# Fourier mixing and a SwiGLU block on one core: the inverse transform's last step by whole blocks of 96 rows, and weight rounding packed into five sixths of each group

## The chip, the cores and the metric

The kernel runs on one core of a Trainium2 chip. The metric is the device time of one execution in microseconds (us). The kernel before takes 2937.25 us, the median of three runs (2936.93 to 2938.33). The profile is of one such execution, with a span of 2935.5 us.

Engines are named as in the profile: PE is TensorE's matmul, PEld its weight load, DVE is VectorE, ACT is ScalarE, POOL is GpSimd, SP is SyncE, which only issues transfers here.

## The reference

Eight batches of 3008 tokens with 256 channels are filtered in the frequency domain along the tokens, and the result goes through a gated feed-forward block.

```python
# x (8, 3008, 256), filt_r and filt_i (1505, 256), all float32
X = np.fft.rfft(x, axis=1)
Y = X * (filt_r + 1j * filt_i)[None]
y = np.fft.irfft(Y, n=3008, axis=1).astype(np.float32)

x2 = y.reshape(24064, 256)
g, val = x2 @ w_gate, x2 @ w_val              # 256 -> 1536
out = ((g / (1 + np.exp(-g))) * val) @ w_out  # 1536 -> 256
```

The weights w_gate, w_val and w_out come as 64-bit floats. The kernel has to turn them into 32-bit floats on the chip, with integer operations on their two halves; its code calls this rounding.

## The kernel before

**Order of work.** The feed-forward part of a batch is 12 steps: 4 chunks of tokens times 3 groups of hidden blocks. One step is one pass through a list of 150 tokens. A token is one small operation, such as a product (P, Q, A, B, E), a copy (m, c, f), a gate (g, u, h, v), a projection (W) or its addition to the output (o). A prime marks work of the group before. The tokens `t0.0` to `t4.2'` advance pieces of the next batch's transforms.

```python
SCHEDULE = """
Q0 o3' t4.2' W2 f0 S00' S01' x0.o' t0.0 x1.o' Q1 t0.1 x2.o' P3 x3.o' f1 t4.3' W1 x4.o' S10' x03 S11'
s13 x5.o' P1 o1 t0.2 P0 o2 c1 D01 A13 g1 c0 S20' Q2 S21' g0 y01 m13 t1.0 h0 f2 s01 W6 t1.1 h1 x23
D02 P2 o6 D12 A01 c2 B13 g2 n3' m01 t0.3 S30' t1.2 x02 W7 S31' g13 y12 y02 B01 h13 o7 t1.3 t2.0 s02
s12 g01 h2 Q3 t2.1 h01 e12 A02 y23 W4 e02 y03 m02 g3 A12 o4 t2.2 E12 m12 B02 t2.3 l12 E02 u12 e13
g02 t3.0 h3 s23 l02 B12 v12 E13 t3.1 h02 u02 A23 n2 l13 g12 v02 W5 s03 e23 h12 e01 m23 A03 o5 u13
E23 t3.2 m03 v13 E01 l23 e03 t3.3 t4.0 l01 u23 B23 v23 u01 t4.1 E03 n1 v01 g23 B03 l03 W3 h23 g03
u03 h03 v03
""".split()
```

Counted from 0, P0 is place 27, A01 place 52, E01 place 127 and v03 place 149. The operations D01, D02, D12 are subtractions on POOL; n2 and n1 make sums for the next chunk on POOL.

**Rounding in the first batch.** All rounding, and the making of further weights as sums of rounded ones, is cut into ticks, numbered 0 to 170. 45 of them are done before the first step. The others are spread over the tokens of the first steps of batch 0. A tick has a few operations: some on DVE and ACT, those on POOL marked below. `finish` runs at the start of a step whatever ticks the step needs that are not yet done.

```python
# round_half(i): one half block of weights
#  n=0 DVE L322 | n=1 DVE L325, ACT L327 | n=2, 3, 4 ACT L330, L332, L334
#  n=5 DVE L337 | n=6 DVE L341
#  n=7 POOL: product with the power of two (L349 into wo_t, or L361 and L362)
#  n=8 POOL: for an output weight, four subtractions
for n, t in enumerate((0, 1, 2, 3, 4, 6, 7, 9, 10)):
    put(b + t, go, by, n > 6)          # b is 48 for the last half that step 1 needs
...                                    # sums of weights for six pairs:
for n, pair in enumerate(PAIRS_USED):  # DVE or ACT, then POOL
    for t in range(3):
        put(b + 11 + n + t, lambda c=c: next(c, None), by if g or n < 4 else 1, t == 2)
```

```python
TICKS = 20
for place, token in enumerate(SCHEDULE):                      # 150 places
    if b == 0 and this and place * TICKS % len(SCHEDULE) < TICKS and \
            (step or place > SCHEDULE.index("A01")):
        preparation.tick(step)
```

The projection `W2` of a step's group stands at place 3 of the next step. Its second half reads the rounded output weights `wo_t` and the last product of the hidden layer, `v03` at place 149.

**The transforms' last step.** A transform along 3008 = 47 x 64 tokens has three stages. Stage 2 leaves its result in DRAM (`d2`), and stage 3 loads it back as `t4` and multiplies it by a small table. One call of `stage3` handles 4 columns of 64 (`NH` = 4) and half of the channels (`cb`), so a chunk has 4 calls and a batch 16. In batch 0 a call is four matmuls over 96 rows with 94 outputs each. From batch 1 on, the rows are stored token by token and packed over 128 partitions, and a call is three matmuls with 141, 188 and 141 outputs.

```python
# L696, batches 1 to 7                       BACK has 3, 4 and 3 pieces of 47 columns
for j in range(len(BACK) if back else 0):
    cols = back_t[0][:, first:first + N1 * len(BACK[j])]
    ...
    pin(nc.tensor.matmul(out=rows, lhsT=self.t4[k, i][:, j, ts(cb, 128)], rhs=cols,
                         start=j == 0, stop=True, skip_group_check=True))
# L699, batch 0
for n in range(0 if back else NH):
    pin(nc.tensor.matmul(out=psv[:, n, :], lhsT=self.t4[k, i][0:NK, n, ts(cb, 128)],
                         rhs=wi_t, start=n == 0, stop=True, skip_group_check=True))
```

```python
# load_t4
t = t4pool.tile([128, NH, C], FP32, ...)
if self.b == 0:
    self.load(out=t[0:NK], in_=self.d2_rows[:, ts(at, NH), :])
else:
    ...
    for j in range(2):
        self.load(out=t[64 * j:64 * j + 64, 1], in_=rows[j, 128 * (1 - j):128 * (1 - j) + 64])
        self.load(out=t[:, 2 * j], in_=rows[j, 64 * j:64 * j + 128])
# stage2b
if self.b == 0:
    pin(queue.dma_start(out=self.twos(self.d2, u), in_=g))
    return
rows = self.d2_tokens.rearrange("n (p s) c -> (n p) (s c)", p=2)
pin(queue.dma_start(out=rows[:, ts(u, NV * C)], in_=g.rearrange("q s c -> q (s c)")))
```

Of the kernel before, what the change touches and what calls it, by code (L numbers as in the profile page):

```python
# [56 lines left out]
NK = 4 * NS  # L57
# [55 lines left out]

BACK = (((0, 0, 0, 48), (1, 48, 0, 48), (2, 96, 0, 32)),
        ((4, 64, 0, 48), (5, 112, 0, 16), (2, 0, 32, 16), (3, 16, 0, 48)),
        ((5, 0, 16, 32), (6, 32, 0, 48), (7, 80, 0, 48)))
BACK_AT = (0, 3 * N1, 7 * N1)


def dft_tables():
    n1, n2 = np.arange(N1), np.arange(N2)
    s, q = np.arange(NS), np.arange(NQ)
    ph = 2 * np.pi * (np.outer(n1, s) % N1) / N1
    w = np.stack([np.cos(ph), -np.sin(ph)], 1)
    wf = np.zeros((N1, 2, NS, 2, 2))
    wi = np.zeros((NS, 2, 2, N1, 2))

    v = np.stack([2 * np.cos(ph), -2 * np.sin(ph)], 0)  # L130
    v[0, :, 0], v[1, :, 0] = 1.0, 0.0
    for h in range(2):
        wf[:, h, :, :, h] = w.transpose(0, 2, 1)
        wi[:, :, h, :, h] = v.transpose(2, 0, 1) / S
    one = wi[:, :, 0, :, 0].transpose(1, 0, 2).reshape(2 * NS, N1)
    back = np.zeros((128, 10 * N1))
    for tile_, first in zip(BACK, BACK_AT):
        for i, (_, row, a, rows) in enumerate(tile_):
            back[row:row + rows, first + N1 * i:first + N1 * (i + 1)] = one[a:a + rows]


    kap = np.where(q[:, None] < 32, s + N1 * q[:, None], s + N1 * (95 - q[:, None]))
    sg = np.where(q < 32, 1.0, -1.0)[:, None]
    th = 2 * np.pi * ((n2[:, None, None] * kap) % S) / S
    c, sn = np.cos(th), np.sin(th)
    d = np.zeros((2, N2, NS, 2, NQ))
    d[0, :, :, 0] = c.transpose(0, 2, 1)
    d[1, :, :, 0] = sn.transpose(0, 2, 1)
    d[0, :, :, 1] = (-sn * sg).transpose(0, 2, 1)
    d[1, :, :, 1] = (c * sg).transpose(0, 2, 1)  # L150
    d = d.reshape(128, NS, 128)
    de = np.stack([d, d.transpose(2, 1, 0)], 2)

    pairs = np.arange(128).reshape(2, N2).T.ravel()
    later = np.stack([de[:, :, 0], de[:, :, 1][:, :, pairs]], 2)
    f32 = np.float32
    return (wf.reshape(NR, NK).astype(f32), wi.reshape(NK, NR).astype(f32),
            back.astype(f32), np.ascontiguousarray(de).astype(f32),
            np.ascontiguousarray(later).astype(f32))
# [3 lines left out]
def kernel(  # L163
# [11 lines left out]
    wf_host, wi_host, back_host, de_host, later_host = dft_tables()  # L175
    wf_dram = nc.inline_tensor(wf_host, name="wf_tbl")
    wi_dram = nc.inline_tensor(wi_host, name="wi_tbl")
    back_dram = nc.inline_tensor(back_host, name="back_tbl")
    de_dram = nc.inline_tensor(de_host, name="de_tbl").ap()
    later_dram = nc.inline_tensor(later_host, name="later_tbl").ap()  # L180
# [292 lines left out]
    back_t = []  # L473

    def load_back():

        t = rpool.tile([128, 2, 128, 2], U32, name="back", tag="raw", bufs=2)
        t = t.bitcast(FP32).rearrange("p b f two -> p (b f two)")
        back_t.append(t[:, 0:10 * N1])
        pin(nc.sync.dma_start(out=back_t[0], in_=back_dram.ap()))  # L480

# [14 lines left out]
    class Spectral:  # L496


        def __init__(self, b):
            self.b = b  # L500
            self.d1, self.d2 = [dram_tiles[2 * (b % 2) + i] for i in range(2)]
            self.d1_rows = self.d1.rearrange("a (h n) c -> (a h) n c", h=2)

            self.d2_tokens = self.d2.rearrange("a n c -> (a n) c").rearrange(
                "(n a) c -> n a c", n=N2)
            self.d2_rows = self.d2.rearrange("a (h n) c -> (a h) n c", h=2)
            self.x, self.t2, self.f, self.tb, self.p, self.t4, self.y = {}, {}, {}, {}, {}, {}, {}
            self.real = {}
# [27 lines left out]
        def load_two(self, u):  # L536
            if u < N_TWO:
                self.tb[u] = lend("tb", u).rearrange("p i (k c) -> p i k c", k=2)
                self.load(out=self.tb[u], in_=later_dram[:, ts(u, NV)])
# [19 lines left out]
        def load_t4(self, k, i, part=None):  # L559
            if part is not None:  # L560

                t = f0[0:NK, ts(i, NH), :]
                r = (slice(0, 64), slice(64, NK))[part]
                self.load(out=t[r], in_=self.d2_rows[r, ts(i, NH), :])
            else:
                t = t4pool.tile([128, NH, C], FP32, name=f"t4_{self.b}_{k}_{i}", tag="t4")
                at = 2 * k + i
                if self.b == 0:
                    self.load(out=t[0:NK], in_=self.d2_rows[:, ts(at, NH), :])
                else:  # L570

                    rows = self.d2_tokens.rearrange("(h n) a c -> h (n a) c", h=2)
                    rows = rows[:, ts(at, 2 * NS * NH)]
                    for j in range(2):
                        self.load(out=t[64 * j:64 * j + 64, 1],
                                  in_=rows[j, 128 * (1 - j):128 * (1 - j) + 64])
                        self.load(out=t[:, 2 * j], in_=rows[j, 64 * j:64 * j + 128])
            self.t4[k, i] = t
# [78 lines left out]
        def stage2b(self, u):  # L657
# [14 lines left out]
            if self.b == 0:  # L672
                pin(queue.dma_start(out=self.twos(self.d2, u), in_=g))
                return
            rows = self.d2_tokens.rearrange("n (p s) c -> (n p) (s c)", p=2)
            pin(queue.dma_start(out=rows[:, ts(u, NV * C)], in_=g.rearrange("q s c -> q (s c)")))

        def stage3(self, k, step):
# [6 lines left out]
            flat = ps.rearrange("p a b -> p (a b)")  # L685
            back = self.b
            for j in range(len(BACK) if back else 0):
                first = BACK_AT[j]
                cols = back_t[0][:, first:first + N1 * len(BACK[j])]

                if j == 1:
                    rows = flat[:, 1:2 * 187 + 1].rearrange("p (z y) -> p z y", z=2)[:, :, ::2]
                else:
                    at = j // 2 * (2 * N1 + 1)
                    rows = flat[:, at:at + 6 * N1 - 1:2]
                pin(nc.tensor.matmul(out=rows, lhsT=self.t4[k, i][:, j, ts(cb, 128)], rhs=cols,  # L696
                                     start=j == 0, stop=True, skip_group_check=True))
            for n in range(0 if back else NH):
                pin(nc.tensor.matmul(out=psv[:, n, :],  # L699
                                             lhsT=self.t4[k, i][0:NK, n, ts(cb, 128)],  # L700
# [352 lines left out]
    chore(NT * NG - 1, "P0", load_back)  # L1053
# [8 lines left out]
    for b in range(B):  # L1062
# [33 lines left out]
        for step in range(NCHUNK * NG + (b == B - 1)):  # L1096
# [4 lines left out]
            if not ghost:  # L1101
# [5 lines left out]
                if b and chunk:  # L1107
                    cur.load_t4(chunk, 0)
# [4 lines left out]
            for place, token in enumerate(SCHEDULE):  # L1113
                if b == 0 and this and place * TICKS % len(SCHEDULE) < TICKS and \
                        (step or place > SCHEDULE.index("A01")):
# [24 lines left out]
                if b and chunk and op == "B01":  # L1140
                    cur.load_t4(chunk, 1)
                for i in range(2):
                    if nxt and (step, op) == (10, ("A12", "E23")[i] if b else "E23"):
# [39 lines left out]
```

## Time and profile before

| | |
|---|---|
| median of three runs | 2937.25 us |
| span of the profiled execution | 2935.5 us |
| PE busy | 2901.7 us (99%) |
| PEld busy | 2805.6 us (96%) |
| DVE busy | 1927.4 us (66%) |
| ACT busy | 1609.7 us (55%) |
| POOL busy | 1579.9 us (54%) |
| moved by DMA | 558.82 MB, mean 190 GB/s |

A float32 matmul of the code stands in the profile as two PE instructions, so counts there are twice those of the code: the 336 matmuls of L696 (3 a call, 16 calls a batch, 7 batches) are listed as 672. The duration of one PE instruction is its latency; matmuls overlap, and how fast they follow each other is read from the chain or from the timeline. In a group's line the columns are line, engine, operation, tiles, shapes and count, then busy time and mean ns of one, then the idle time of the engine ahead of it.

The steps of batch 0 that hold rounding run from about 78 us to 297 us of the span, some 30 us each.

### The profile page before, as it was taken

To read this page: it belongs to the slowest core of one execution; us is meant where nothing else is said; L and a number is where in the kernel's file an instruction comes from. 1 tells how busy PE (TensorE), PEld (TensorE's weight loads), DVE (VectorE), ACT (ScalarE), POOL (GpSimd) and SP (SyncE) were. 2 spreads that over 40 slices of the span, in tenths; PEclk is the share of its full clock that TensorE was granted. 3 is DMA by queue.
4 is the path that set the end of the run, shared out by engine and by line. 5 is a ranking of instruction groups with operands and counts; after the bars stand their busy time and mean duration, and the time that the engine had idled before them with its cause. 6 is when DMAs were issued, how large, how long until landed. Compare 5 with 4: busy or idle time off the path is not lost.

```text
span 2935.5 us, 57365 instructions
## 1 busy us (share of the span) xinstructions
PE 2901.7 (99%) x20040; PEld 2805.6 (96%) x20040; DVE 1927.4 (66%) x4384; ACT 1609.7 (55%) x4208; POOL 1579.9 (54%) x1759
## 2 busy tenths in 40 slices
PE   7999999999999999999999999999999999999999
PEld 5889999999999999999999999999999999999999
DVE  6888765576655676557765667656666566666665
ACT  6775455555555555555455554555555555555554
POOL 3876655556444655456554556454564545555453
PEclk9999999999999999999999999999999999999999
DMA  8677855575555755556646566556665566644442
GB/s 227 213 258 250 304 189 179 179 229 180 179 182 186 223 186 166 189 183 205 213 155 193 184 203 211 164 177 203 194 199 173 177 208 194 200 139 154 148 130 88
DMA packets 225661, 558.82 MB, mean 190 GB/s; under 512 B 32666, under 2 KB 110474, under 8 KB 225374
## 3 DMA queue, kind: packets, MB, share of 16 engines
q1 hardware_dynamic: 190286, 485.84, 52.6%
q10 hardware_dynamic: 26160, 45.43, 4.3%
q0 software_dynamic: 8928, 23.89, 2.3%
q8 instruction: 161, 2.64, 0.4%
q14 instruction: 126, 1.03, 0.1%
HBM read 459.97 MB, written 95.05 MB: 189 GB/s over the span
## 4 chain that ended last, share of the span: by engine, by line
PE 94%; DVE 1%; POOL 1%; ACT 0%; issue 0%; DVEq 0%; POOLq 0%
PE wa L791 24%; PE wA L870 17%; PE wk L791 16%; PE we L791 12%; PE wG L870 9%; PE wF L870 4%; PE pa L590 3%; PE pd L696 3%; PE pc L662 2%; PE pb L630 2%; PE pd L699 0%; POOL y_t L245 0%; DVE h L838 0%; POOL wt_t L245 0%; POOL wt_t L248 0%
## 5 line engine op out<-in xcount | busy, mean ns | idle before, releaser
L791 PE MATMUL wa<-y_t,wt_t 128*128 128x188 f32 x4464 | 878.8, 323 | 3.8 <-issue 1.4
L791 PEld LDWEIGHTS wa<-y_t,wt_t 128*128 128x128 f32 x4464 | 730.2, 190 | 28.6 <-issue 17.3
L245 POOL TENSOR_TENSOR h<-h 128x376 f32<-128x376 f32 x190 | 182.8, 983 | 779.2 <-DVE h L838 779.2
L870 PE MATMUL wA<-wo_t,h 128*128 128x128 f32 x4608 | 576.9, 275 | 2.3 <-DVE o L245 1.7
L870 PEld LDWEIGHTS wA<-wo_t,h 128*128 128x128 f32 x4608 | 563.0, 192 | 16.3 <-issue 10.8
L791 PE MATMUL wk<-y,wt_t 128*128 128x188 f32 x2976 | 566.2, 323 | 0.0
L248 POOL TENSOR_TENSOR h<-h 128x376 f32<-128x376 f32 x570 | 554.8, 995 | 0.5
L791 PEld LDWEIGHTS wk<-y,wt_t 128*128 128x128 f32 x2976 | 479.1, 190 | 25.9 <-issue 19.8
L248 DVE TENSOR_TENSOR we<-we,m 128x376 f32<-128x376 f32 x576 | 318.4, 556 | 195.2 <-PE we L791 134.1
L791 PE MATMUL we<-y_t,wt_t 128*128 128x188 f32 x2232 | 431.5, 323 | 1.4 <-ACT we L822 1.4
L791 PEld LDWEIGHTS we<-y_t,wt_t 128*128 128x128 f32 x2232 | 369.4, 190 | 1.8 <-ACT we L822 1.7
L248 POOL TENSOR_TENSOR D<-f,f 128x376 f32<-128x376 f32 x288 | 280.7, 988 | 103.3 <-ACT f L806 102.6
L252 DVE SCALAR_TENSOR_TENSOR y<-wk,c 128x376 f32<-128x376 f32 x480 | 244.8, 542 | 131.4 <-ACT we L822 55.0
L826 ACT COPY m<-wa 128x376 f32<-128x376 f32 x576 | 272.0, 472 | 87.1 <-PE wa L791 85.9
L833 ACT ACTIVATE g<-wa 128x188 f32<-128x188 f32 x576 | 187.9, 326 | 187.5 <-PE wa L791 180.0
L870 PE MATMUL wG<-wo_t,h 128*128 128x128 f32 x2304 | 288.3, 275 | 0.6 <-DVE o L245 0.6
L870 PEld LDWEIGHTS wG<-wo_t,h 128*128 128x128 f32 x2304 | 281.4, 192 | 0.8 <-DVE o L245 0.8
L833 ACT ACTIVATE u<-we 128x188 f32<-128x188 f32 x576 | 188.9, 328 | 168.2 <-DVE we L248 149.9
L806 ACT ACTIVATE f<-wk 128x376 f32<-128x376 f32 x288 | 139.4, 484 | 234.4 <-PE wk L791 213.2
L810 ACT COPY c<-wk 128x376 f32<-128x376 f32 x288 | 136.0, 472 | 226.1 <-PE wk L791 226.1
L813 DVE SCALAR_TENSOR_TENSOR x<-wk,f 128x376 f32<-128x376 f32 x192 | 104.3, 543 | 234.4 <-PE wk L791 228.6
L822 ACT COPY we<-y 128x376 f32<-128x376 f32 x480 | 224.1, 487 | 32.9 <-DVE h L838 14.2
(144 smaller groups left out, 3893.8 us busy)
## 6 DMA issues: line engine op xcount, KB each, us to landing
wt_t<-w_all SPq DMA_DIRECT2D x174, 896.0 KB
wt_t<-w_all SPq DMA_DIRECT2D x174, 768.0 KB
d<-t ACTq DMA_DIRECT2D x112, 192.0 KB
lent<-later_tbl SPq DMA_DIRECT2D x84, 256.0 KB
lent<-in_filt_r_dram SPq DMA_DIRECT2D x336, 64.0 KB
lent<-d SPq DMA_DIRECT2D x84, 256.0 KB
d<-lent ACTq DMA_DIRECT2D x84, 256.0 KB
x<-in_x_dram SPq DMA_DIRECT2D x112, 160.0 KB
```

Of the source, the lines that this page charges most:

```text
L245: return eng.tensor_tensor(out=dst, in0=a, in1=b, op=ALU.add)
L248: return eng.tensor_tensor(out=dst, in0=a, in1=b, op=ALU.subtract)
L252: return nc.vector.scalar_tensor_tensor(out=dst, in0=a, scalar=-1.0, in1=b, op0=ALU.mult, op1=ALU.subtract)
L590: pin(nc.tensor.matmul(out=ps[0:NK], lhsT=wf_t, rhs=self.x.pop(u), start=True, stop=True))
L791: pin(nc.tensor.matmul(out=ps[:, z], lhsT=self.wt[:, SLOT[p], z], rhs=rhs, start=start and z == 0, stop=True, skip_group_check=True))
L806: pin(act.mul(self.small(f"f{i}", f"f{i}", 1), t[f"k{i}"], -1.0))
L810: pin(act.copy(out=self.small(f"c{i}", f"c{i}", 1), in_=t[f"k{i}"]))
L813: pin(v.scalar_tensor_tensor(out=dst, in0=t[f"k{j}"], scalar=-1.0, in1=t[f"f{i}" if j == 3 else f"D{at}"], op0=ALU.mult, op1=ALU.add))
L822: pin(act.copy(out=self.bank(f"e{at}"), in_=t[f"y{at}"]))
L826: pin(act.copy(out=self.small(f"m{at}", "m", 4), in_=t[f"a{at}"]))
L833: pin(act.activation(out=self.small(op, "g", 3, 1)[:, 0], in_=ps[:, 1], func=AF.Silu))
L870: pin(nc.tensor.matmul(out=self.tiles[at][:, t, :], lhsT=self.hs[i][:, HID[p], t0:t0 + 128], rhs=wo_t[:, JB * q + i, WO[p], :], start=star ...
```

## The change

It has two parts that do not touch each other.

**Stage 3** of batches 1 to 7 is written as in batch 0: rows stay in 96 partitions, four matmuls of 94 outputs a call, one load a tile in place of four. The table `back`, its load, the reordered table `later` and the stores by tokens go away. The two loads of a chunk are issued together at the start of its step (before, the second one waited for token B01, and in step 10 for E23).

**Rounding in batch 0** gets the same 20 ticks a step, but they are spread over the first 127 of the 150 places, so that no tick stands after E01. In step 0 ticks begin after P0 and not after A01. This leaves the end of each step to the feed-forward's own operations.

```diff
@@ stage3
-            for j in range(len(BACK) if back else 0):
-                first = BACK_AT[j]
-                cols = back_t[0][:, first:first + N1 * len(BACK[j])]
...
-                pin(nc.tensor.matmul(out=rows, lhsT=self.t4[k, i][:, j, ts(cb, 128)], rhs=cols,
-                                     start=j == 0, stop=True, skip_group_check=True))
-            for n in range(0 if back else NH):
+            for n in range(NH):
                 pin(nc.tensor.matmul(out=psv[:, n, :],
-                                             lhsT=self.t4[k, i][0:NK, n, ts(cb, 128)],
+                                             lhsT=self.t4[k, i][:, n, ts(cb, 128)],
                                              rhs=wi_t, start=n == 0, stop=True,
                                              skip_group_check=True))
@@ load_t4
-                t = t4pool.tile([128, NH, C], FP32, name=f"t4_{self.b}_{k}_{i}", tag="t4")
...
-                    for j in range(2):
-                        self.load(out=t[64 * j:64 * j + 64, 1],
-                                  in_=rows[j, 128 * (1 - j):128 * (1 - j) + 64])
-                        self.load(out=t[:, 2 * j], in_=rows[j, 64 * j:64 * j + 128])
+                t = t4pool.tile([NK, NH, C], FP32, name=f"t4_{self.b}_{k}_{i}", tag="t4")
+                self.load(out=t, in_=self.d2_rows[:, ts(2 * k + i, NH), :])
@@ stage2b
-            if self.b == 0:
-                pin(queue.dma_start(out=self.twos(self.d2, u), in_=g))
-                return
-            rows = self.d2_tokens.rearrange("n (p s) c -> (n p) (s c)", p=2)
-            pin(queue.dma_start(out=rows[:, ts(u, NV * C)], in_=g.rearrange("q s c -> q (s c)")))
+            pin(queue.dma_start(out=self.twos(self.d2, u), in_=g))
@@ the loop over steps
                 if b and chunk:
-                    cur.load_t4(chunk, 0)
+                    for i in range(2):
+                        cur.load_t4(chunk, i)
...
-                if b == 0 and this and place * TICKS % len(SCHEDULE) < TICKS and \
-                        (step or place > SCHEDULE.index("A01")):
+                span = SCHEDULE.index("E01")
+                if b == 0 and this and place < span and place * TICKS % span < TICKS and \
+                        (step or place > SCHEDULE.index("P0")):
                     preparation.tick(step)
...
-                if b and chunk and op == "B01":
-                    cur.load_t4(chunk, 1)
-                for i in range(2):
-                    if nxt and (step, op) == (10, ("A12", "E23")[i] if b else "E23"):
+                if nxt and (step, op) == (10, "A12" if b else "E23"):
+                    for i in range(2):
                         nxt.load_t4(0, i)
```

## The prediction

> **What bounds the kernel now.** I read the page first (busy time, then the chain), then the busy time by stretches, then TensorE's waits in the one stretch where it idles, then single pieces of the chain and groups by shape, to get the spacing of matmuls.
>
> ```profile
> PE 2901.7 (99%) x20040; PEld 2805.6 (96%) x20040; DVE 1927.4 (66%) x4384; ACT 1609.7 (55%) x4208; POOL 1579.9 (54%) x1759
> ```
> ```profile
> core 0: us, PE busy (x) PEld busy (x) DVE busy (x) ACT busy (x) POOL busy (x), PEclk, DMA share, GB/s
> 77.50:400.00 322.50, 311.25 (x2091) 294.96 (x2090) 259.00 (x567) 200.99 (x548) 229.93 (x285) 0.99 0.77 255
> 400.00:2905.00 2505.00, 2505.00 (x17447) 2441.08 (x17446) 1597.46 (x3678) 1351.94 (x3543) 1321.47 (x1432) 1.00 0.57 183
> 2905.00:2935.50 30.50, 23.93 (x182) 23.16 (x180) 17.81 (x42) 8.06 (x23) 0.00 (x0) 0.98 0.08 26
> ```
>
> From 400 to 2905 us PE is busy in all 2505.00 us, and the list of its waits in that stretch is empty. There the time is the sum of the spacings of PE's instructions and nothing else: a matmul more or less is paid in full, and whatever happens on DMA, DVE, ACT or POOL costs nothing until it makes PE wait. Only batch 0 (77.5 to 400 us) has idle time of PE, 322.50 - 311.25 = 11.25 us. Its causes:
>
> ```profile
> PE wF L870 <- POOL wo_t L349: 2.6, 1, 2.6
> PE wF L870 <- DVE h L838: 1.5, 1, 1.5
> PE wa L791 <- issue: 1.4, 1, 1.4
> PE we L791 <- ACT we L822: 1.4, 1, 1.4
> PE wa L791 <- ACT m L826: 1.2, 2, 1.0
> ```
>
> The first two are the projection W2 at the start of a step. It waits for a rounded weight at 107.7 us and for the last hidden product at 174.5 us. So the stage 3 part of the change acts where PE has no slack, and the rounding part acts on at most these 11 us and what they do to the clock.
>
> **What the Trainium skill says.** (1) "TensorE: Matmul & The Clock Gate", section "LDWEIGHTS (loading the stationary operand)": a weight load takes columns / 1.2 ns, and the number of rows does not matter; for 128 columns, 107 ns as an estimate. Its section "Back-to-back issue gap" says that spacing in a stream of loads and matmuls is set by both. The trace agrees in kind. Twelve instructions of 128 outputs take 1.34 us in the chain, 112 ns each, and the first batch's L699, with 94 outputs and 96 rows, comes out at the same spacing below: a floor near a weight load. The page's N/2.4 + 2.5 ns for long matmuls does not hold for this float32: 188 outputs would be 81 ns, and the chain shows 1.27 / 8 = 159 ns.
> (2) The same page, "What's actually happening": after an idle window of some 3.4 us the array runs at half clock. The trace shows it after the wait at 107.7 us: eight L699 matmuls take 1.65 us there and 0.86 us elsewhere, and the stretch 104 to 139.2 us has a granted clock of 0.95.
> (3) "SBUF — State Buffer", "SBUF: two separate sides": DVE with two SBUF inputs and POOL lock one pair of ports, and the loser waits. The trace fits: in 77 to 180 us L337 on DVE, one shape, takes 407 to 1143 ns.
>
> **Part one, stage 3: PE.** The pieces of the chain give one call of each kind, and what follows it (columns: start us, length us, what):
>
> ```profile
> 419.57 0.81 PE pd L696 x6
> 420.37 1.27 PE wk L791 x8
> ...
> 116.78 0.86 PE pd L699 x8
> 117.64 1.37 PE wA L870 x12
> ```
> ```profile
> L696 PE MATMUL pd<-back,t 128*128 128x141 f32 x448 | 90.4, 283 | 0.0
> L696 PE MATMUL pd<-back,t 128*128 128x188 f32 x224 | 54.1, 322 | 0.0
> ...
> L699 PE MATMUL pd<-wi_t,t 96*128 96x94 f32 x96 | 13.2, 283 | 0.0
> ```
>
> An old call is 6 instructions: 420.37 - 419.57 = 0.80 us, which is two of 188 outputs at 0.159 and four of 141 at 0.12. A new call is 8 instructions in 0.86 us, and the group after it takes 1.37 where 12 such usually take 1.34, so 0.89 us, 8 x 0.111. The difference is 0.09 us a call. There are 16 calls in each of 7 batches, 112: **+10.1 us**, all on the path. The new form streams fewer outputs (8 x 94 = 752 against 940 instruction outputs a call) but loads weights eight times and not six, and each of the eight sits on the floor of 111 ns.
>
> **Part one: transfers.** Four loads a tile become one, with packets of 4 KB for 1 KB; stores go the other way, from 2 KB to 1 KB. The bytes are the same. DMA is busy 57% in the stretch 400 to 2905 us and PE never waits. Both loads of a chunk now start at the start of its step, while the first use of chunk 1 stands at place 71 of 150, nearly half a step (some 14 us) later. I put the effect at 0.
>
> **Part two, rounding.** Before, a tick stands every 150 / 20 = 7.5 places; after, every 127 / 20 = 6.35 places up to place 121. Counting places in step 0: before, 13 ticks (numbers 45 to 57) from place 53 to 143, and number 58 as a burst at the start of step 1; after, 15 ticks (45 to 59) from place 32 to 121. The product that W2 of step 1 waits for is tick 57, since its half has base 48 and POOL's product is 9 ticks on. It moves from place 143 to 108, and so from behind the sums n1 and n2 on POOL to ahead of both:
>
> ```profile
> 105.31 1.42 POOL L245 TENSOR_TENSOR y_t<-y_t,y 128x564 f32<-128x564 f32 x1
> 106.69 0.96 POOL L349 TENSOR_TENSOR wo_t<-wo_t,pw 128x256 f32<-128x256 f32 x1
> ```
> ```profile
> 104.49 1.01 DVE L325 TENSOR_SCALAR pw<-wo_t 128x256 uint32<-128x256 uint32 x1
> ...
> 106.40 0.34 DVE L838 TENSOR_TENSOR h<-we,u 128x188 f32<-128x188 f32 x1
> ```
>
> In the POOL lines y_t is the tail of n1 and wo_t is that product. It should come some 7 us sooner (35 places of a step of some 28 us). The second line pair shows DVE's queue at the same time: the last hidden product ends at 106.7 us, behind rounding operations of 1 us that go away from this place. Worth: the wait of 2.6 us and the slow clock behind it (5% of 35.2 us, 1.8 us), together **-4.4 us**. The wait at 174.5 us for DVE's last product goes the same way: **-1.5 us**.
>
> What it costs: the same DVE work in less time. In the step from 104 us DVE is busy 28.62 of 35.20 us. Of that, four rounding lines (L322, L325, L337, L341: 2.67 + 3.34 + 4.00 + 4.15) are 14.2 us. In five sixths of the step (29.3 us) there would be 14.2 + 14.4 x 5/6 = 26.2 us, 89% against 81% now. In the same stretch of steps 1 to 3 some pieces will come late; I choose +1.6 us, about the one wait of 1.4 us for ACT that such a crowd made at 167 us. And in step 0 ticks 45 and 46, some 4 us of POOL work (two pairs of weight sums and a product, each operation 0.7 to 0.9 us), now stand between D01 and D02. D12 then comes at about 92 us; DVE used it at 91.1 us. I choose +1.5 us. Part two together: -4.4 - 1.5 + 1.6 + 1.5 = **-2.8 us**.
>
> **The sum**: 2937.25 + 10.1 - 2.8 = 2944.6 us; I say 2944.
>
> **Rivals.** (a) Spacing goes by outputs streamed, not by weight loads: then a call falls by 188 instruction outputs, 0.159 us, and 112 calls give -17.8 us, 2917 with part two. For it: 141, 188, 256 outputs lie on a line. Against it: 94 and 128 outputs both show 111 to 112 ns. I give it 2%. (b) Crowding: DVE and POOL become the bound in steps 0 to 3, the ends of steps gain nothing, and PE's waits grow by 5 us: 2952. For it: 89% on DVE and locked ports. Against it: between 80 and 86 us DVE idles 1.10, 0.93 and 1.59 us in its timeline, which the new early ticks can fill. 12%. (c) Rounding removes nearly all of PE's idle time in batch 0, 9 us: 2938. For it: most of these waits stand near rounding operations. Against it: several have other causes, such as the sums' chain at the start. 15%. (d) A transfer makes PE wait from batch 1 on, because two t4 loads stand ahead of a weight reload in SP's queue: +3 us or more. Against it: the waits are empty now, and a step's reload has most of a step. 4%.
>
> **Range and chances.** Part one is sure to about 1 us, since both forms are in the trace. Part two may lie between -7 and +4. That gives 2939 to 2950. 2% are 59 us, far outside every rival: within 2% 0.99, the rest on both sides.
>
> **What would show it.** Right: L699 listed with about 1024 instructions, spacing 111 ns, none of L696, and PE still without idle time from 400 us on, with that stretch 10 us longer; no wait of wF for wo_t near 107 us; some new waits for D or for DVE between 85 and 100 us or in the middle of steps 1 to 3. Wrong: idle time of PE in batches 1 to 7, a spacing of L699 other than 111 ns, or waits in batch 0 that sum to more than 15 us or less than 5.

## The result, and the profile after

The changed kernel takes 2956.35 us (median, 2955.94 to 2964.53) against 2937.79 us of the kernel before on the same chip: 1.0067 [1.0048, 1.0087], 18.6 us more, where 2944 had been predicted. (Such a figure is the ratio to the kernel before on the same chip, with its 95% interval.) The same kernel once more gave 2956.73 us and 1.0059 [1.0044, 1.0074]; that second trace (called "changed again" below) is the one compared step by step. In some executions PE's clock is at half before the first step (in the changed kernel's first trace for 13.65 us from 72.4 us on, in "changed again" for 3.41 us from 72.8 us on) and all that follows is later, 7.1 and 1.8 us here, so pieces are compared by their length and not by their place.

Line numbers move with the change: products L791 are L732, the projection L870 is L811, stage 3 (L696 and L699) is L640, rounding L322 to L349 is L302 to L329, the sums and subtractions on POOL L245 and L248 are L225 and L228.

The page of the changed kernel, busy time:

```profile
PE 2921.1 (99%) x20264; PEld 2823.2 (95%) x20264; DVE 1932.7 (65%) x4384; ACT 1612.8 (54%) x4208; POOL 1581.2 (53%) x1759
```

PE has 224 instructions more, which are 112 calls of two more each. The stretch from batch 1 on, columns as in the prediction:

```profile
400.00:2905.00 2505.00, 2505.00 (x17592) 2440.86 (x17591) 1590.82 (x3658) 1345.36 (x3523) 1322.47 (x1435) 1.00 0.58 184
```

PE is again busy in all 2505.00 us. One call of the new form, from the chain of waits of the changed kernel (start us, length us, what):

```profile
434.86 0.86 PE pd L640 x8
435.72 1.30 PE wk L732 x8
...
440.91 0.86 PE pd L640 x8
441.78 1.37 PE wA L811 x12
```

and its groups by shape, in which no line with 141 or 188 outputs of `back` is left:

```profile
L640 PE MATMUL pd<-wi_t,t 96*128 96x94 f32 x992 | 128.2, 272 | 0.0
L640 PE MATMUL wpd<-wi_t,f 96*128 96x94 f32 x32 | 7.0, 419 | 0.0
```

Eight instructions in 0.86 us, and the follower a little longer (1.37 and 1.30 us), are what the prediction read from batch 0. From the projection W2 of step 11 on, where every batch but the first runs, the changed kernel takes 2512.3 us in both its traces, the kernel before 2501.9: **+10.4 us**.

The rest is in batch 0. The length of a step is taken from the first product of W2 to that of the next W2; step 0 begins with the first gate or value product. All in us:

| step | 0 | 1 | 2 | 3 | 4 | 5 | 6 | step 11's W2 to the last W2 |
|---|---|---|---|---|---|---|---|---|
| before | 26.4 | 35.2 | 32.7 | 32.0 | 30.2 | 30.5 | 31.8 | 2501.9 |
| changed again | 30.2 | 31.9 | 38.3 | 30.5 | 30.2 | 32.6 | 31.9 | 2512.3 |
| difference | +3.8 | -3.3 | +5.6 | -1.5 | 0 | +2.1 | +0.1 | +10.4 |

With a start 1.8 us later and 0.3 us in later steps these make the 19.3 us between the spans (2954.8 and 2935.5). Stage 3, step 1 and step 3 did what was predicted. Steps 0, 2 and 5 did not. PE's waits in batch 0 of "changed again" (total us, times, longest us):

```profile
PE wa L732 <- ACT m L767: 4.1, 3, 2.1
PE wa L732 <- POOL y_t L225: 2.6, 2, 1.9
PE we L732 <- DVE we L232: 1.4, 1, 1.4
PE wA L811 <- POOL D L228: 1.4, 1, 1.4
...
PE wF L811 <- DVE h L779: 0.3, 1, 0.3
```

The wait of W2 (tile wF) for wo_t, 2.6 us before, is gone, and that for h fell from 1.5 to 0.3 us. Those for the copy `m` grew from 1.2 to 4.1 us. The wait of 1.9 us for a y_t sum of POOL is in step 0; the kernel before has one of 1.40 us at the same place, listed under "issue". Of the waits for `m`, those of 2.12 and 0.91 us stand in step 2, and the first is followed back here. Five lines of "changed again" from the timelines of PE, ACT, DVE and POOL, in that order (start us, length us, what; in brackets the idle time before and what ended it):

```profile
163.16 0.90 PE L732 MATMUL wa<-y_t,wt_t 128*128 128x188 f32 x4 [2.12 <-ACT m L767]
...
161.92 0.42 ACT L307 ACTIVATE w<-w 128x256 f32<-128x256 uint32 x1 [2.00 <-DVE w L302]
...
161.09 0.80 DVE L302 TENSOR_SCALAR w<-wo_t 128x256 uint32<-128x256 uint32 x1 [1.31 <-POOL lent L225]
...
158.31 2.33 POOL L228 TENSOR_TENSOR h<-h 128x376 f32<-128x376 f32 x2
160.60 0.45 POOL L225 TENSOR_TENSOR lent<-w,lent 128x128 f32<-128x128 f32 x1
```

PE waits for `m`. ACT had stood for 2.00 us at a rounding operation ahead of `m` in its queue. That one waited for DVE's first operation of the same half, which waited for the buffer `w`, and POOL let go of that only behind 2.33 us of two subtractions of h. A wait of one engine's background work is handed to the next because the kernel keeps each engine's operations in program order (`pin` in the code). The clock then adds to it (stretches of 2 us of "changed again"):

```profile
162.00:164.00 2.00, 0.84 (x5) 0.84 (x6) 2.00 (x4) 1.11 (x3) 2.00 (x4) 1.00 0.86 284
...
168.00:170.00 2.00, 1.17 (x4) 1.17 (x5) 2.00 (x5) 0.42 (x2) 2.00 (x4) 0.60 0.00 0
170.00:172.00 2.00, 2.00 (x10) 2.00 (x9) 2.00 (x5) 1.37 (x4) 2.00 (x4) 0.55 0.12 10
172.00:174.00 2.00, 1.37 (x12) 1.21 (x11) 2.00 (x7) 1.20 (x3) 1.92 (x4) 1.00 0.91 222
```

The first wait alone leaves the clock at 1.00. After two more, of 0.91 us and 1.44 us, it is 0.60 and 0.55 for two stretches. At a slow clock of half (0.50 in 104 to 106 us of the same trace), that is (0.40 + 0.45) x 2.00 / 0.5 = 3.4 us at half clock, which cost 1.7 us.

### The profile page after: what moved, and what is told of

Its sections match the earlier page's. It is cut to its first block, busy times and chain, and to the rows that moved or that the text cites. A ratio compares the mean times of both kernels' runs of the same rounds, so it can differ in the third digit from the quotient of the medians.

```text
span 2961.2 us, 57634 instructions
## 1 busy us (share of the span) xinstructions
PE 2921.1 (99%) x20264; PEld 2823.2 (95%) x20264; DVE 1932.7 (65%) x4384; ACT 1612.8 (54%) x4208; POOL 1581.2 (53%) x1759
## 4 chain that ended last, share of the span: by engine, by line
PE 93%; POOL 1%; DVE 1%; DMA 1%; ACT 0%; issue 0%; POOLq 0%; DVEq 0%
PE wa L732 24%; PE wA L811 17%; PE wk L732 16%; PE we L732 12%; PE wG L811 8%; PE wF L811 4%; PE pd L640 3%; PE pa L548 3%; PE pc L620 2%; PE pb L588 2%; POOL h L228 0%; DMA d<-lent 0%; POOL D L228 0%; DMA lent<-d 0%; POOL lent L225 0%
## 5 line engine op out<-in xcount | busy, mean ns | idle before, releaser
L732 PE MATMUL wa<-y_t,wt_t 128*128 128x188 f32 x4464 | 881.7, 323 | 9.8 <-POOL y_t L225 3.4
L732 PEld LDWEIGHTS wa<-y_t,wt_t 128*128 128x128 f32 x4464 | 730.6, 190 | 35.4 <-issue 14.2
L225 POOL TENSOR_TENSOR h<-h 128x376 f32<-128x376 f32 x190 | 183.0, 984 | 803.7 <-DVE h L779 794.1
L811 PE MATMUL wA<-wo_t,h 128*128 128x128 f32 x4608 | 578.0, 275 | 4.0 <-DVE o L225 1.8
L811 PEld LDWEIGHTS wA<-wo_t,h 128*128 128x128 f32 x4608 | 563.0, 192 | 17.9 <-issue 10.7
L732 PE MATMUL wk<-y,wt_t 128*128 128x188 f32 x2976 | 567.6, 323 | 0.3 <-ACT f L747 0.3
L228 POOL TENSOR_TENSOR h<-h 128x376 f32<-128x376 f32 x570 | 555.5, 996 | 0.5
L732 PEld LDWEIGHTS wk<-y,wt_t 128*128 128x128 f32 x2976 | 479.1, 190 | 26.8 <-issue 20.8
L228 DVE TENSOR_TENSOR we<-we,m 128x376 f32<-128x376 f32 x576 | 318.4, 556 | 200.6 <-PE we L732 142.0
L732 PE MATMUL we<-y_t,wt_t 128*128 128x188 f32 x2232 | 433.1, 324 | 1.0 <-DVE we L232 0.9
L732 PEld LDWEIGHTS we<-y_t,wt_t 128*128 128x128 f32 x2232 | 371.2, 191 | 1.6 <-DVE we L232 1.5
L228 POOL TENSOR_TENSOR D<-f,f 128x376 f32<-128x376 f32 x288 | 280.3, 986 | 104.4 <-ACT f L747 103.7
L811 PE MATMUL wG<-wo_t,h 128*128 128x128 f32 x2304 | 288.3, 275 | 0.6 <-DVE o L225 0.6
L811 PEld LDWEIGHTS wG<-wo_t,h 128*128 128x128 f32 x2304 | 281.4, 192 | 0.8 <-DVE o L225 0.8
```

Of the source, the lines that this page charges most:

```text
L225: return eng.tensor_tensor(out=dst, in0=a, in1=b, op=ALU.add)
L228: return eng.tensor_tensor(out=dst, in0=a, in1=b, op=ALU.subtract)
L732: pin(nc.tensor.matmul(out=ps[:, z], lhsT=self.wt[:, SLOT[p], z], rhs=rhs, start=start and z == 0, stop=True, skip_group_check=True))
L811: pin(nc.tensor.matmul(out=self.tiles[at][:, t, :], lhsT=self.hs[i][:, HID[p], t0:t0 + 128], rhs=wo_t[:, JB * q + i, WO[p], :], start=star ...
```

## The experiments

**The two parts apart.** Theory: stage 3 costs 10 us by itself and all the rest comes from where rounding stands. Rival: the new loads of stage 3 disturb the weight reloads of batch 0.

e1 is the changed kernel with the ticks of before:

```diff
-                span = SCHEDULE.index("E01")
-                if b == 0 and this and place < span and place * TICKS % span < TICKS and \
-                        (step or place > SCHEDULE.index("P0")):
+                if b == 0 and this and place * TICKS % len(SCHEDULE) < TICKS and \
+                        (step or place > SCHEDULE.index("A01")):
```

> Stage 3 as in the changed kernel, rounding spread as in the kernel before. If the two parts are independent and stage 3 costs its weight loads (8 instructions at 112 ns against 6 that take 0.80 us a call, 112 calls), this is +10 us on the kernel before, about 2948 us, with all of it between 400 us and the end and no idle time of PE there. If stage 3 also slows something by its transfers, the sum is larger and idle time of PE shows up after 400 us.

Measured: 2955.0 us (2947.76 to 2956.51), 1.0044 [1.0029, 1.0058]. From step 11 on 2512.3 us, the same 10.4 us as in the whole change, and no wait of PE in

```profile
400.00:2905.00 2505.00, 2505.00 (x17591) 2441.07 (x17590) 1592.16 (x3664) 1348.00 (x3531) 1314.22 (x1424) 1.00 0.58 183
```

In the trace 1.9 us more lie in step 1 and 1.1 us in step 8, the other steps stand within 0.4 us of before. Traces with the old stage 3 show the same: e18 has 36.7 us in step 1, with the same short waits of PE for ACT and DVE, and step 8 takes 31.0 to 33.9 us among them; e6 has 32.8 us there, with PE's wait of 1.0 us for a load of `lent` as in e1. So the new loads are not needed to explain these 3 us. The shortest of the five runs is the 2948 us that the 10 us give; three are at 2955 to 2956.5 us and lift the median.

e2 is the kernel before with the new ticks, the same edit the other way round:

> Rounding packed into five sixths as in the changed kernel, stage 3 as in the kernel before. If the missing time of the change lies in the rounding part, this is +8 us, about 2946 us, most of it in the third step (index 2, where the changed kernel's step took 40.0 us against 32.7). If the rounding part is worth the predicted -2.8 us, this is about 2935 and stage 3 must cost twice as much as counted. The start of the kernel (up to the first product, some 78 us) should be as before; the changed kernel's profile has it 7 us later, which I take for that execution's own.

Measured: 2946.08 us (2944.47 to 2953.83), 1.0020 [1.0012, 1.0029]. Its steps 0 to 5 are 28.4, 32.7, 40.0, 30.5, 30.2 and 32.5 us, to 0.1 us those of the changed kernel's first trace, which began as late, and from step 11 on it has the 2501.9 us of before. The parts add: 1.0044 and 1.0020 make 1.0064. These intervals are wide (that of e1 is 8.5 us); the step lengths are the firmer ground. The rounding part, predicted at -2.8 us, costs about 6 to 7, and step 2 alone has 7.3 us more.

**Is it the buffer `w`?** By the chain above, yes: one more buffer should remove the wait. It has two buffers besides places lent out by a larger tile; e3 gave every third half a place at the end of that tile, e5 a tile of its own.

```diff
+        elif i % 3 == 1 and i < N_LENT:
+            w = lent[:, NPR * 256:NPR * 256 + 256]...      # e3
+            w = tail[:, 0:256]...                          # e5: a tile of its own
+            w = tail[:, ts(i // 3 % 2, 256)]...            # e9: two places in turn
```

> As e2, but the rounded mantissas w rotate over four buffers and not three (a fourth in an unused end of an SBUF tile). Theory of the queue: POOL frees a w buffer late, DVE's next rounding operation waits for it in order, ACT's waits behind that, and the copy that PE waits for stands behind that; then a fourth buffer takes 3 to 6 us from step 2 and the time is about 2941. Theory of throughput: DVE and POOL simply have too much to do in five sixths of the step; then the time stays at e2's within 1.5 us.

Measured: 2947.38 us, 1.0025 [1.0015, 1.0034]; step 2 takes 38.9 us.

> As e3, but the fourth w buffer is a tile of its own. In e3 DVE still waited 1.3 us for POOL ahead of a write into the fourth buffer, which lay in a tile that holds weights too, so e3 did not take the wait away. Theory of the queue: with the buffer really free, DVE's rounding operation at the middle of step 2 no longer waits for POOL, PE's wait of 2.1 us for ACT's copy m goes with the half clock behind it, and step 2 falls from about 39 to 36 us or less: about 2942 us. Theory of throughput: step 2 stays within 1 us of e3's 38.9 and the time at about 2946.

Measured: 2946.99 us, 1.0026 [1.0014, 1.0038]; step 2 takes 38.3 us. Neither removed the wait: half 22 took the place of half 19, which was in use. So both say nothing on the theory. e9 gives these halves two places in turn.

> As e2, with the w buffers of two thirds of the weight halves alternating between two places each. In e3 and e5 the half that waited (number 22) still took the place of number 19, because each residue of three kept one place; so both left the wait in. Theory of the queue: now DVE's rounding operation some 20 us into step 2 does not wait 1.3 us for POOL, PE's wait of 2.3 us for ACT's copy goes, and step 2 falls from 38 to 40 us to 36 or less; about 2942 us. If DVE is then just as late through its own work, PE's wait stays above 1.5 us and the time at 2945 to 2947.

Measured: 2945.31 us (2941.81 to 2951.43), 1.0026 [1.0015, 1.0038]. PE's first wait for `m` in step 2 became shorter, 1.43 us for 2.10 us in e2, but a second one of 0.65 us came up, that for `we` grew from 0.94 to 1.46 us, and step 2 takes 38.7 us. DVE now reaches the rounding operation without idle time, from other background work (weight sums of 0.83 and 0.91 us), and ACT still stands 1.31 us behind it. The buffer was where the wait passed through, not its cause.

**Is it the density?** This is the prediction's term for crowding: 20 ticks in 127 places and not in 150. e4 spreads them over the whole of step 2 and leaves the rest of e2.

```diff
-                span = SCHEDULE.index("E01")
+                span = len(SCHEDULE) if step == 2 else SCHEDULE.index("E01")
```

> As e2, but in step 2 alone the ticks are spread over the whole list as before. Theory of density: the loss of step 2 is made by packing there, so step 2 is some 7 us shorter and the wait of the next step's W2 for the last product (1.5 us) comes back: about 2940 us. If the loss comes from ticks being ahead because step 0 did two more of them (a shift by one tick in which work falls on step 2), the spread of step 2 alone recovers less than half.

Measured: 2941.05 us (2940.05 to 2941.63), 1.0004 [0.9996, 1.0013]; step 2 takes 33.7 us. That fits density, but e4 also moves every tick of step 2 later. The next three part the two. e10 keeps the new density in step 2 and starts 23 places later:

```diff
+                at = place - 23 if step == 2 else place
+                if b == 0 and this and 0 <= at < span and at * TICKS % span < TICKS and ...
```

> As e2, but in step 2 the same packed ticks (one every 6.35 places) stand 23 places later, from place 23 to 144. The density is that of the changed kernel, but the run of weight sums for six pairs starts at place 68 or later, as in the kernel before. Theory of density: step 2 stays at 38 us or more, and W2's wait at the start of step 3 comes back: 2946 or more. Theory of place: what counts is which operations the run of sums meets; step 2 falls to about 34 us and the time to 2941.

Measured: 2943.03 us, 1.0016 [1.0009, 1.0023]; step 2 takes 33.3 us, at the full density of the change.

e8 keeps the old density everywhere and only starts step 0's ticks earlier, so that those of steps 1 and 2 come two ticks (15 places) sooner:

```diff
-                        (step or place > SCHEDULE.index("A01")):
+                        (step or place > SCHEDULE.index("P0")):
```

> The kernel before with one half of the rounding part alone: ticks in step 0 begin after P0, but are spread over the whole list in all steps. The output weight that W2 of step 1 waits for is then at place 120 and not 143. If the early start gives the gain at W2 and density the loss, steps 0 and 1 together are 2 to 4 us shorter than before and step 2 stays near 33: about 2935 us. If the early start itself costs (weight sums on POOL ahead of D02 and D12), step 0 grows by 3 to 5 us and the gain is eaten: 2938 us or more.

Measured: 2943.44 us, 1.0020 [1.0014, 1.0027]; step 2 takes 38.0 us, at the old density.

e11 does the same to step 2, with step 0 and step 1 left as they were:

```diff
                     preparation.finish(step)
+                    preparation.tick(step, 2 * (step == 2))
```

> The kernel before, with two more ticks at the start of step 2, so that the rounding of step 2 runs two ticks (15 places) earlier, at the old density. Theory of density: nothing changes but the burst itself, below 1 us: 2938 to 2939. Theory of place: the run of sums starts at place 45 to 60 as in the changed kernel and in e8, and step 2 grows from 32.7 to about 37 us: 2942.

Measured: 2943.11 us, 1.0012 [1.0004, 1.0019]; step 2 takes 36.5 us. e14 is the opposite, one tick later than before:

```diff
+                        (step or place > SCHEDULE.index("A01")) and (step, place) != (1, 0):
```

> The kernel before with one tick less in step 1, so that rounding in step 2 runs one tick (7.5 places) later than before; the opposite of e11. Theory of place, if later is better throughout: step 2 falls below 32.7, about 32 us, and the time to 2937. If the kernel before already stands at the best place, step 2 or the start of step 3 grows by 1 to 2 us: 2939 to 2940.

Measured: 2942.31 us, 1.0012 [1.0005, 1.0019]; step 2 takes 36.2 us, 3.5 more than before, where at most 2 were expected.

To compare them, take six ticks as a mark of where the run of rounding stands: the sums of weights of the second group that go to POOL. My expectations counted them as ticks 89 to 94; they are 93 to 98, and the places here are counted anew.

| kernel | density in step 2 | the six sums at places | step 2, us | lost to half clock | the rest |
|---|---|---|---|---|---|
| e14 | old | 113 to 143, the sixth in step 3 | 36.2 | 0 | 36.2 |
| before | old | 105 to 143 | 32.7 | 0 | 32.7 |
| e10 | new | 106 to 138 | 33.3 | 0 | 33.3 |
| e4 | old | 98 to 135 | 33.7 | 0 | 33.7 |
| e11 | old | 90 to 128 | 36.5 | 0 | 36.5 |
| e8 | old | 90 to 128 | 38.0 | 1.7 | 36.3 |
| changed again | new | 83 to 115 | 38.3 | 1.7 | 36.6 |
| e2 | new | 83 to 115 | 40.0 | 3.4 | 36.6 |

The last columns take off half of the time in which the granted clock is 0.50: 3.41 us in e8 and in "changed again", twice that in e2. What is left is the same to 0.3 us in the last four lines, at either density.

Step 2 by busy time, of the kernel before, then of e10, e11 and "changed again", one fence each (stretch, length, then busy us of PE, PEld, DVE, ACT, POOL, with counts):

```profile
139.90:172.60 32.70, 30.87 (x224) 29.83 (x223) 28.22 (x62) 23.30 (x64) 29.06 (x40) 1.00 0.73 244
```
```profile
140.30:173.70 33.40, 31.42 (x225) 29.90 (x223) 28.27 (x62) 23.50 (x64) 29.51 (x42) 1.00 0.70 225
```
```profile
146.10:182.60 36.50, 32.70 (x224) 29.97 (x223) 32.78 (x70) 25.52 (x72) 32.70 (x45) 1.00 0.70 225
```
```profile
142.20:180.50 38.30, 33.09 (x224) 31.40 (x223) 32.54 (x67) 25.39 (x69) 32.21 (x45) 0.96 0.63 203
```

PE has 224 or 225 instructions in each. At the same density the step is good or bad by where the ticks stand, and at the same places it is good at either density. **Density falls as the cause of step 2, and place stands**: which operations of the step a stretch of rounding meets. More of the rounding also falls inside a slow step (67 to 70 operations of DVE for 62), but that alone does not make it slow: e4 has 67 too and takes 33.7 us, and e14 has 65 and takes 36.2. Packing is then one of the ways to move the place. The early start puts step 2 of the changed kernel one tick ahead of the kernel before, which does one tick more in step 1, and that alone costs 1.0 us (e4). Packing moves the six sums from 98 to 135 on to 83 to 115. The kernel before stands at the best of those tried, with a loss on both sides. In e11 the loss sits in no single wait: PE's idle time grows by 2.0 us over several short ones (the longest new one is 0.7 us, for `m`), and its busy time by 1.8 us at full clock, which stays open. The columns also show what I had passed over: POOL, not DVE, was the fullest beside PE in the kernel before, 29.06 of 32.70 us.

**Is it the sums on POOL?** e6 puts the sums of the second group on POOL five ticks later (in e2), e15 does so in the kernel before, and e7 moves E sums of this group from POOL to DVE (in e2).

```diff
-                            put(b + 11 + n + t, lambda c=c: next(c, None),
+                            put(b + 11 + n + t + (5 if g == 1 and t == 2 else 0),      # e6, e15
+                                lambda c=c: next(c, None),
-   pin(add(nc.vector if early else nc.gpsimd, wt_f...
+   pin(add(nc.vector if early or g == 1 else nc.gpsimd, wt_f...                        # e7
```

> As e2, but POOL's twelve weight sums of step 2 (6 pairs, 0.7 to 0.9 us each) stand five ticks later, at places 89 to 121 and not 58 to 89. If POOL's order in the middle of step 2 is the cause, step 2 falls by 3 us or more: about 2942. If DVE's load is the cause, nothing changes in the middle and POOL may be late at the end of the step: 2945 to 2948.

Measured: 2941.8 us, 1.0011 [1.0004, 1.0018]; step 2 takes 36.2 us, 2.1 to 3.8 less than in the runs with the new ticks (38.3 and 40.0), and step 3 32.5 us, 2.0 more. The shift went further than I had counted: the sums of four of the six pairs leave step 2 and come as a burst at the start of step 3, and every later tick stands four sooner. Step 5 then takes 28.5 us and not 32.5.

> The kernel before, with POOL's twelve weight sums of step 2 five ticks later (places 113 to 150). In e6 the same shift left step 5 without its waits (28.5 us against 30.5 before). If that was the shift's doing, this is faster than the kernel before by 1 to 3 us (2935 to 2937). If the sums now meet n1 on POOL at the end of step 2 and hold up step 3, it is 2938 to 2940.

Measured: 2940.7 us, 1.0003 [0.9994, 1.0011]; step 2 takes 31.1 us and not 32.7, but step 3 37.9 and not 32.0, because five of the sums then come as a burst at its start. POOL in step 2 has 24.17 us for 29.06:

```profile
141.20:172.30 31.10, 30.70 (x224) 29.80 (x223) 26.76 (x62) 23.17 (x65) 24.17 (x36) 1.00 0.77 253
```

> As e2, but six of the twelve weight sums of step 2 go from POOL to DVE: POOL loses 6 x 0.8 = 4.8 us, DVE gains 6 x 0.4 to 0.9, some 4 us. If POOL bounds step 2, it gets shorter by 2 us or more (about 2943). If DVE bounds it, it gets longer by 2 to 4 us (about 2949).

Measured: 2945.39 us, 1.0028 [1.0018, 1.0038]; step 2 takes 37.9 us. Sums on POOL are a part of step 2's loss, some 2 us of the 3.9 us that are not slow clock (e6 without its 1.7 us of slow clock is 34.5 us), and on DVE they do hardly better (36.2 us without it). What the rest meets I could only argue from the chain above: rounding operations that stand in ACT's and DVE's queues ahead of `m` and `we`.

**Step 0.** The prediction's cause was that weight sums would stand ahead of D02 and D12 on POOL. e12 (e2 with the first group's later sums four ticks later) takes them away:

```diff
+                            put(b + 11 + n + t + 4 * (g == 0 and n > 3 and t == 2), ...
```

> As e2, but the four weight sums on POOL that fell between D01 and D02 in step 0 stand four ticks later, behind D12. If POOL's sums ahead of D02 and D12 are what the early start costs, the waits at A02 and A12 in step 0 go and step 0 falls by 2 to 3 us: about 2943. If step 0 is held up by something else (PE's wait of 2.8 us for the sums y_t at the end of step 0), it stays at 2945 to 2946.

Measured: 2947.5 us, 1.0033 [1.0021, 1.0045]; PE's wait of 1.50 us for D in e2 is gone and D02 starts 3.0 us sooner in its step than in "changed again" (7.9 and 10.9 us after the first product), but step 0 is no shorter than there, 30.2 us. The wait near its end is still there in e12, and longer:

```profile
PE wa L792 <- POOL y_t L245: 3.3, 2, 2.8
```

So D was not what step 0 hung on. POOL's sums for that y_t in e12 themselves begin only after 1.80 us of idle, when ACT's copy of y_t comes, so POOL's load at that place is not the cause either. The copy stands in ACT's queue close behind a rounding operation that had waited 0.64 us for DVE's first one; what else makes ACT late there is not settled.

**The changed kernel again**, for a second trace:

> The changed kernel once more. In its first profile the first product of the feed-forward part started at 85.4 us, against 78.3 us in the kernel before, which is the code of neither part. If that was this execution's own, the time is again 2956 us and a profile with a start near 78 us shows steps 0 to 6 together 8 us longer than before, with step 2 at 38 to 40 us.

Measured: 2956.73 us (2955.25 to 2957.84). Its numbers are those used above.

**Can place be turned into a gain?** Three on the kernel before. e16 takes four more ticks in step 4, so that step 5's come earlier. e17 takes one tick ahead of n1 in step 0, so that W2's wo_t comes in time. e18 does both.

```diff
+                if b == 0 and this and step == 4 and place in (20, 55, 90, 125):       # e16, e18
+                    preparation.tick(step)
+                if b == 0 and this and step == 0 and token == "n1":                    # e17, e18
+                    preparation.tick(step)
```

> The kernel before, with four more ticks in step 4 (which has no waits), so that steps 5 and 6 run four ticks earlier at the old density, as they did in e6 and e15. Theory of place: step 5 falls from 30.5 to about 28.5 us as there, and the time by 2 us to about 2936. If step 5's gain in e15 had another cause, step 5 stays at 30.5 and the time within 0.5 us.

Measured: 2936.24 us (2934.45 to 2943.43), 0.9995 [0.9987, 1.0003]. Step 5 takes 28.6 us for 30.5, as place would have it (e6 has 28.5 at the new density, e15 28.5 at the old), step 4 30.7 for 30.2; the interval includes no change.

> The kernel before, with one tick more in step 0, just ahead of n1, and hence none at the start of step 1; all later steps keep their places. The product that W2 waits for stands ahead of n1's three sums on POOL (4.1 us). If POOL's order alone makes W2's wait of 2.75 us with 1.5 us of half clock behind it, step 1 falls from 35.2 to 32 or 33 us (DVE's last product still ends 1.8 us late) without step 0's growth in the changed kernel: about 2935.5. If the sums of n1 are then what step 1 waits for, the gain is below 1 us.

Measured: 2938.45 us, 0.9998 [0.9990, 1.0006]. W2 of step 1 still waits 2.15 us, now for the last h of DVE (v03).

> e16 and e17 together. The two act in different steps, so their gains should add: about 2933 to 2934 us, faster than the kernel before and the changed kernel. If the shift in step 4 depends on how step 1 ended, less.

Measured: 2936.9 us, 0.9994 [0.9985, 1.0002]. None of the versions is clearly faster than the kernel before.

## Why the prediction was wrong, point by point

- **Stage 3 on PE, +10.1 us: right.** +10.4 us, 0.093 us for each of 112 calls and not 0.09. Counts, form and follower are as read from batch 0. Rival (a), time by outputs streamed, is refuted.
- **Transfers, 0: right** from batch 1 on. PE does not wait there in either trace of the changed kernel, nor in e1; rival (d) is refuted.
- **W2 of step 1, -4.4 us: right in mechanism**, -3.3 us measured. The wait for wo_t is gone. e17 shows that moving the product alone would not have done: DVE's tail has to go too, which the five sixths also did. **W2 of step 3, -1.5 us: right**, -1.5 us.
- **Crowding, "I choose +1.6 us": this step failed.** It measured +5.6 us in step 2 and +2.1 us in step 5, which the prediction had left out, together 7.7. It was sized as throughput, by how full DVE would be in five sixths of a step. e10 packs the ticks as tightly and takes 33.3 us, and e8 and e11 don't and take 38.0 and 36.5. What costs is the place: the early start (one tick in step 2) and above all the packing bring its six sums from places 105 to 143 to 83 to 115, onto other operations, and 3.9 of the 5.6 us are that. Step 5 goes by place too (28.5 us in e6 with the ticks as tight but four further ahead, for 32.5 in e2). The prediction followed the moving of ticks in step 0, for the one that helped, and not in the steps after it. It also took the price of a new wait as the wait alone, though it had charged the slow clock to the old one: in step 2 PE's idle time grew by 3.4 us (38.30 - 33.09 against 32.70 - 30.87) and its busy time, for the same instructions, by 2.2 us, most of it at half clock.
- **Step 0, +1.5 us: too small, and its cause fell.** +3.8 us measured. 1.7 us are a stretch of half clock after the wait for y_t, and PE's idle time grew from 3.3 to 4.9 us; the wait for y_t is 1.9 of these, for 1.4 before. D, the cause named, does come late (DVE stands 0.87 us for it in "changed again"), but in e12 it came sooner without gain, since the wait for y_t then grew to 2.75 us.
- **The sum of rounding, -2.8 us**, became +6 to +7 us by e2. Rival (b) came closest in size (2952), but with the wrong mechanism, and rival (c) is refuted: PE's idle time in batch 0 grew from 11.25 to 15.4 us, over the 15 us that the prediction had named as a sign against it. Rounding was allowed +4 us at most, on the strength of that one choice. (2937.25 + 10.1 + 4 is 2951 and not the 2950 at which the range ends; the time lies outside either.) The last 2 us are a later start: 3.41 us of half clock from 72.8 us on, ahead of the first step. e14 and e15, with the old ticks there, have such a stretch too and start at 80.6 and 80.1 us, so it says nothing of the change.

## What to carry to other kernels

Where PE never waits, the cost of another matmul form can be read from one call of each form and its follower: 10.1 us came out for 10.4. A form with fewer outputs lost here, since more weight loads came with it and an instruction of 94 outputs still took 0.111 us. Background work cut into ticks and pushed into the ordered queues of a tight schedule is not a load to be averaged: shift it by 15 places and look, on every step that follows, at which foreground operations stand behind it and on which engine it waits itself. Allow for a slow clock behind each cluster of waits on PE (0, 1.7 or 3.4 us in step 2 of these runs), and judge such a change by step lengths, not by the first wait that disappears.

## What the runs showed that was not expected

- **The slow clock came in units of 3.41 us, each at a cost of 1.7 us**: one after the wait of 2.58 us in the kernel before, one after the 1.91 us for y_t in "changed again" (0.88, 0.50 and 0.76 in three stretches of 2 us), one after three waits of 2.12, 0.91 and 1.44 us within 8 us, and four in a row, 13.65 us, ahead of the first step in the changed kernel's first trace. The Trainium skill, "TensorE: Matmul & The Clock Gate", "What's actually happening", has the clock fall after at least one idle window of about 3.4 us. The length agrees; in the first three cases no single wait was as long as that before the fall. The falls of one trace also lie whole units apart: in "changed again" at 72.82, 103.54 and 168.39 us, which is 9 and 19 times 3.413 us. So the same wait can cost more or less by when it comes: the wait of 2.12 us for `m` in "changed again" left the clock at 1.00, and that of 2.10 us at the same place of e2 was followed by a fall within 0.5 us.
- **A shift of 15 places ahead at the same density makes step 2 3.8 to 5.3 us longer** (e11 and e8), and one of a single tick back makes it 3.5 us longer (e14).
- **Packets of 4 KB in place of 1 KB for the loads of stage 3 made no difference to PE**: DMA is busy 58% (57% before) in the stretch from 400 us on, and PE idles 0 us there with either.
